# Two linear-attention branches under one gate: pk^T x of both branches as one 2x2 block product with seven block products

## The chip, the cores and the metric

The kernel runs on one core of a Trainium2 chip. The metric is the device time of one execution in microseconds. The engines are named as the profile names them: PE multiplies matrices (PEld is its weight load), DVE does vector arithmetic, ACT activations and copies, POOL little here, and SP issues nearly all DMAs. SBUF is the memory that all engines and the DMAs reach, PSUM the one that matmuls write into.

## The reference

```python
x = A_x                                        # 2048 x 640; B_x is not used
g = sigmoid((x * gate_w).sum(-1, keepdims=True))
def branch(x, wqkv, wo):                       # S=2048, D=640, H=32 heads of Dh=20
    q, k, v = split_heads(x @ wqkv)
    phi = lambda t: where(t > 0, t + 1, exp(t)) + 1e-6
    pq, pk = phi(q), phi(k)
    kv  = einsum("bhsd,bhse->bhde", pk, v);  z = einsum("bhsd->bhd", pk)
    num = einsum("bhqd,bhde->bhqe", pq, kv); den = einsum("bhqd,bhd->bhq", pq, z) + 1e-6
    return merge_heads(num / den) @ wo
out = g * branch(x, A_wqkv, A_wo) + (1 - g) * branch(x, B_wqkv, B_wo)
```

All inputs and the output are bf16. Both branches have the same x, so v is never formed: the kernel computes G = pk^T x (640 x 640 for each branch), and from it kv = G Wv, of which only the diagonal blocks of the heads are kept. The small kv and Wo are multiplied to one matrix W' for each branch, so that out = (pqA, scaled) W'A + (pqB, scaled) W'B.

## The kernel before, in words

Everything is laid out in SBUF by `body`, which builds a list of operations, each with an engine, a planned cost, its inputs and outputs, and a priority. A planner (`Sched`, L77 to L256) then walks through a modelled time: PE's operations keep the order in which the program lists them, the operations of the other engines are taken by the earliest modelled start and then by priority, and this order is emitted. Each engine then works through its own fixed list, waiting on semaphores. PSUM has eight banks of 512 fp32 columns, which the planner hands out (pool "ps").

The stages, in PE's order:

- **Loads** (L425 to L457, one SP queue in the program's order; x's tile 1 and the gate weights go by ACT's). The key weights, x transposed (XT, DMA transposes), x in rows (XN, with a column of ones behind its 640 columns), then WQ, WV and WO of both branches, and the constants CST last. WO is loaded in pieces of 60 partitions (L444 to L451).
- **Keys** (L592 `k_both`, for tiles 2 to 15 of 128 rows). One tile of both branches takes three PSUM banks: 512 columns of A, the last 128 of A and B together with a gate column, 512 of B. That is 15 matmuls at L613. ACT takes exponentials (L626, L630, L667); DVE clamps them (L640) and adds max(k, 0) from PSUM (L650). The result pk goes to PKS.
- **G and queries** (L713 `g_unit`, L870 `q_unit`). For each branch and each of five column groups g, 16 row tiles are accumulated: a matmul of 512 columns (L720) and one of 129 (L721; the last column is x's ones column, which gives z). Between them lie query units: five matmuls of 512 columns (L874), an exponential and a relu on ACT (L891, L898), a clamp and an addition on DVE (L901, L909). All of branch A is done before branch B. A G group is copied by ACT (L729) and transposed by a DMA on SP's queue into GS (L739).
- **Denominators** (L923 `t_sum`, L950 `den`). DVE multiplies pq by z and sums over five groups (L932, L935), a DMA transposes the sums, DVE reduces four rows to one (L969), takes the reciprocal (L981) and multiplies by the gate (L984), a DMA transposes back, and DVE scales pq (L1013). This is done in 512-row blocks b = 0 to 3 and for each branch by itself.
- **kv and W'** (L754 `kv_unit`, L804 `wp_burst`). kv is 30 matmuls for a branch (L782), masked by DVE into KVL (L762). A W' burst is half of the columns (L817), copied by ACT (L832); after the second half five DMAs store W' to memory (L854) and one reads it back in another layout (L846).
- **Output** (L1026 `o_mm`). 16 tiles; a tile has 10 matmuls of 512 columns and 10 of 128 for the two branches (L1034). For 15 tiles the part of branch A is done first (L1054 `o_part`), stored as fp32 by ACT, and added by DVE to the part of branch B (L1060 `o_rest`, L1071). The last tile is accumulated in PSUM. One DMA stores each tile.

The order around the change is written out by hand in L1119 to L1185: the fills of the B groups with queries, kv and W' of A inside B's G groups, the 15 `o_part` of A around kv and W' of B, and four `behind` relations.

```python
for g in range(NC):                        # L1119
    g_unit("A", g, lambda k: q_next(1))
...
for g in range(NC):                        # L1151
    g_unit("B", g, fill_b(g))
    q_next((2, 2, 1, 0, 0)[g])
...
l = PKt[X][:, t, g::5]                     # L719
e.matmul(a[:, 0:512], l, XN[:, t, 0:512], start=(t == 0), stop=(t == NT - 1))
return e.matmul(a[:, 512 : D + 1], l, XN[:, t, 512 : D + 1], start=(t == 0), stop=(t == NT - 1))
```

Of the kernel before, what the change touches and what calls it, by code (L numbers as in the profile page):

```python
# [39 lines left out]
XS_W = 672  # L40
KB_W = 648

# [222 lines left out]
def body(nc, A_x, A_wqkv, A_wo, B_x, B_wqkv, B_wo, gate_w, out, log=None):  # L265
# [11 lines left out]
    WKW = sb("WKW", [128, 2 * NU * D], bf)  # L277
    WKC = WKW[:, 0 : NC * 2 * KB_W].rearrange("p (c x f) -> p c x f", c=NC, x=2)
    WK = {X: WKC[:, :, i, :] for i, X in enumerate(XS)}
    WQ = {X: sb("WQ" + X, [128, NC, D], bf) for X in XS}  # L280
    WV = {X: sb("WV" + X, [128, NC, D + 28], bf) for X in XS}
    WO = {X: sb("WO" + X, [128, NU, D], bf) for X in XS}
    PKS = sb("PKS", [128, 2, NT * D], bf)
    PK = {X: PKS[:, i, :] for i, X in enumerate(XS)}
    PKt = {X: PK[X].rearrange("p (t f) -> p t f", t=NT) for X in XS}
    EX = [sb("EX%d" % i, [128, NC, 512], bf) for i in range(3)]

    def slot(X, i):
        return PK[X][:, 2560 * i : 2560 * i + 2560].rearrange("p (g s) -> p g s", g=NC)

    PQ = {
        ("A", 0): EX[0],
        ("A", 1): EX[1],
        ("A", 2): EX[2],
        ("A", 3): slot("A", 0),
        ("B", 0): slot("A", 1),
        ("B", 1): slot("A", 2),
        ("B", 2): slot("A", 3),
        ("B", 3): None,
    }  # L300
    GTS = {X: WKW[:, i * NU * D : i * NU * D + NC * D].rearrange("p (g f) -> p g f", g=NC) for i, X in enumerate(XS)}
    GS = {X: sb("GS" + X, [128, NC, D], bf) for X in XS}
    KVL = {X: sb("KVL" + X, [128, NU, GR], bf) for X in XS}
    WST = {X: WKW[:, i * NU * D : (i + 1) * NU * D].rearrange("p (u f) -> p u f", u=NU) for i, X in enumerate(XS)}
    WP = {X: sb("WP" + X, [128, NC, D], bf) for X in XS}
    XNf = XN[:, :, :].rearrange("p t f -> p (t f)")
    GSf = GS["A"][:, :, :].rearrange("p c f -> p (c f)")
    PQ["B", 3] = GSf[:, 0:2560].rearrange("p (g s) -> p g s", g=NC)
    FXT = {"A": WV["A"][:, :, :].rearrange("p c f -> p (c f)")[:, 0:2048].rearrange("p (b s) -> p b s", b=NB), "B": XNf[:, 0:2048].rearrange("p (b s) -> p b s", b=NB)}
    NOA = 15  # L310
    OA = [XNf[:, 2048 + 1280 * i : 3328 + 1280 * i].bitcast(f32) for i in range(6)]
    OA += [PK["B"][:, 1280 * i : 1280 * i + 1280].bitcast(f32) for i in range(8)]
    OA += [XT[:, :, :].rearrange("p c s -> p (c s)")[:, 0:1280].bitcast(f32)]
    NEK, NEQ, NOS = 4, 4, 4
    EK = sb("EK", [128, NEK, D], bf)
    EQ = EK[:, :, :].rearrange("p k f -> p (k f)")[:, 0 : NEQ * 512].rearrange("p (k f) -> p k f", k=NEQ)
    TSB = sb("TSB", [128, NB * 1024], bf)
    OST = TSB[:, 0 : NOS * D].rearrange("p (k f) -> p k f", k=NOS)
    TSF = [TSB[:, 1024 * b : 1024 * b + 1024].bitcast(f32) for b in range(NB)]
    TSH = sb("TSH", [128, NB, 512], bf)  # L320
    ZC = sb("ZC", [128, 2 * NC], f32)
    DNT = sb("DNT", [128, NB, 128], f32)
    TTR = sb("TTR", [128, NB, 4, 128], bf)
    FF = sb("FF", [128, NB, 512], bf)
# [3 lines left out]
    GG = sb("GG", [128, 2, NT], f32)  # L328
    ONE = sb("ONE", [128, 2], bf)
    SCR = sb("SCR", [128, 1], f32)  # L330
    EPSC = sb("EPSC", [128, 1], f32)
    PS = nc.alloc_psum_tensor("ps", [128, 8, 512], f32)


    IDN = sb("IDN", [128, 128], bf)
# [3 lines left out]
    sch = Sched({"ps": 8, "ek": NEK, "eq": NEQ, "os": NOS})  # L339
# [29 lines left out]

    def dve4(n):  # L370
        return 150 + 0.27 * n
# [25 lines left out]
    bpad = {X: Buf("pad") for X in XS}  # L397
    for X in XS:
        for lo, hi in ((0, 4), (D + 4, D + 28)):
            op("POOL", lambda e, X=X, lo=lo, hi=hi: e.memset(WV[X][:, :, lo:hi], 0.0), 300.0, outs=[bpad[X]], prio=10**6, name="wvpad")  # L400
    bxo = Buf("xo")
    op("POOL", lambda e: e.memset(XN[:, :, D : D + 1], 1.0), 200.0, outs=[bxo], name="xones")
# [36 lines left out]
    for X in XS:  # L439
        dma("SP", "wv" + X, WV[X][:, :, 4 : D + 4], w3(X, 2), 819200, outs=[bwv[X]])  # L440
    for X in XS:
        for r in range(2):
            bwo[X, r] = Buf("wo")
            dma(  # L444
                "SP",
                "wo%s%d" % (X, r),
                WO[X][4 + HR * r : 64 + HR * r, 0:5, :],
                wo[X][0:600, :].rearrange("(u r p) n -> r p u n", r=2, p=HR)[r],
                384000,
                outs=[bwo[X, r]],  # L450
            )  # L451
        bwo[X, 2] = Buf("wo")
        dma("SP", "wopad" + X, WO[X][0:4, 0:5, :], wo[X][0:4, :].unsqueeze(1).to_broadcast([4, 5, D]), 25600, outs=[bpad[X]])
        dma("SP", "wo2" + X, WO[X][64:104, 5, :], wo[X][600:640, :], 51200, outs=[bwo[X, 2]])

    dma("SP", "cst", CST[:, :], cap[:, :], 128 * CW * 2, outs=[bcst])
    loading.clear()  # L457


# [50 lines left out]
    def gate_col():  # L510
        bt = Buf("gwp", "ps")

        def tv():
            return PS[:, bt.slot, 0:NC]

        op("PE", lambda e: e.matmul(tv(), GWZ[:, :], IDN[:, 0:NC], start=True, stop=True), 60.0, ins=[bgw, bid], outs=[bt], name="gwt")
        op(
            "DVE",
            lambda e: e.tensor_copy(WKC[:, :, :, D : D + 1], tv().unsqueeze(2).unsqueeze(3).to_broadcast([128, NC, 2, 1])),
            170.0,  # L520
            ins=[bt],
            outs=[bgc],
            name="gwc",
        )


    bpk = {}

# [21 lines left out]
    def k_post(X, t, ps):  # L550
        ek = Buf("ek", "ek")
        ek2 = Buf("ek2")
        pk = Buf("pk%s%d" % (X, t))
        bpk[X, t] = pk
        first = []
        if X == "B":
            b = Buf("ge")
            bge.append(b)
            op(
                "ACT",  # L560
                lambda e: e.activation(GE[:, t : t + 1], psw(ps, D + 1)[:, D : D + 1], ACT.Exp, scale=-1.0),
                200.0,
                ins=[ps],
                outs=[b],
                name="ge",
            )
            first = [b]
        op("ACT", lambda e: e.activation(EK[:, ek.slot, :], psw(ps, D), ACT.Exp), act_cost(D), ins=[ps] + first, outs=[ek], name="ke")
        op(
            "DVE",  # L570
            lambda e: e.tensor_scalar(EK[:, ek.slot, :], EK[:, ek.slot, :], 1.0, EPS, op0=ALU.min, op1=ALU.add),
            dve4(D),
            ins=[ek],
            outs=[ek2],
            name="kt",
        )
        op(
            "DVE",
            lambda e: e.scalar_tensor_tensor(PKt[X][:, t, :], psw(ps, D), 0.0, EK[:, ek.slot, :], op0=ALU.max, op1=ALU.add),
            dve1(D),  # L580
            ins=[ps, ek, ek2],
            outs=[pk],
            name="ks",
        )

    def k_unit(X, t):
        ps = Buf("k", "ps", 2)
        for c in range(NC):
            k_step(X, t, c, ps)
# [635 lines left out]
```

## Time and profile before

| what | us |
|---|---|
| time, median of 3 runs (lowest, highest) | 187.42 (187.31, 187.66) |
| span of the profiled execution, the time that the profile gives of it | 186.2 |
| first matmul of the key tiles from 2 on (L613) | 10.36 |
| first matmul of the G groups (L720) | 48.33 |
| first output matmul (L1034) | 137.88 |
| last engine instruction (DVE, L1078) starts | 184.17 |
| PE busy in these three stretches, 10.36:48.33, 48.33:90.00, 108.00:137.88 | 37.76, 41.41, 29.67 |
| DVE busy in the same | 32.34, 23.93, 28.01 |
| ACT busy in the same | 24.47, 21.26, 20.42 |

How to read it: the span goes from the first to the last instruction of the profiled execution; the time of a run is a little longer than the span. An engine's busy time is the union of its instructions. A matmul's length in the profile holds the way through the array, which the next matmul overlaps, so the distance from one start to the next tells what it costs. The chain of work that ended last goes back from the last instruction, at each step to what released it. A group of instructions is one source line with one operation and, by shape, one form; "idle before" is the time for which its engine had nothing to do just before, with the engine and line that ended it.

### The profile page before, as it was taken

To read this page: it belongs to the slowest core of one execution; us is meant where nothing else is said; L and a number is where in the kernel's file an instruction comes from. 1 tells how busy PE (TensorE), PEld (TensorE's weight loads), DVE (VectorE), ACT (ScalarE), POOL (GpSimd) and SP (SyncE) were. 2 spreads that over 40 slices of the span, in tenths; PEclk is the share of its full clock that TensorE was granted. 3 is DMA by queue.
4 is the path that set the end of the run, shared out by engine and by line. 5 is a ranking of instruction groups with operands and counts; after the bars stand their busy time and mean duration, and the time that the engine had idled before them with its cause. 6 is when DMAs were issued, how large, how long until landed. Compare 5 with 4: busy or idle time off the path is not lost.

```text
span 186.2 us, 3116 instructions
## 1 busy us (share of the span) xinstructions
PE 182.4 (98%) x1204; PEld 105.8 (57%) x1227; DVE 137.2 (74%) x278; ACT 96.6 (52%) x181; POOL 1.1 (1%) x12
## 2 busy tenths in 40 slices
PE   9999999999999999999999999999999999999995
PEld 4555555555655556555556555555566555555553
DVE  2289888888733555487989899999899998159563
ACT  5265656666554546544675666888623784400001
POOL 2000000000000000000000000000000000000000
PEclk9999999999999999999999999999999999999999
DMA  7979999998006011010501402115515246622324
GB/s 225 268 150 144 273 364 369 353 179 159 4 0 39 0 35 35 4 35 6 114 0 39 84 10 56 32 43 168 178 39 118 58 77 175 189 74 110 138 108 141
DMA packets 36501, 21.37 MB, mean 115 GB/s; under 512 B 25694, under 2 KB 36230, under 8 KB 36486
## 3 DMA queue, kind: packets, MB, share of 16 engines
q1 hardware_dynamic: 36188, 20.97, 44.9%
q10 hardware_dynamic: 298, 0.20, 0.4%
q8 instruction: 9, 0.15, 0.3%
q14 instruction: 6, 0.05, 0.1%
HBM read 10.87 MB, written 4.26 MB: 81 GB/s over the span
## 4 chain that ended last, share of the span: by engine, by line
PE 93%; SPq 3%; DMA 2%; issue 1%; DVE 0%; DVEq 0%
PE ps L1034 23%; PE ps L874 23%; PE ps L613 20%; PE ps L720 18%; PE ps L721 5%; SPq L353 3%; DMA XT<-in_A_x_dram 2%; PE ps L782 2%; PE ps L817 1%; PE ps L535 0%; PE ps L536 0%; DVE TSB L1078 0%; DVEq L237 0%
## 5 line engine op out<-in xcount | busy, mean ns | idle before, releaser
L720 PE MATMUL ps<-XN,PKS 128*128 128x512 bf16 x154 | 45.8, 379 | 0.1
L891 ACT ACTIVATE EK<-ps 128x512 bf16<-128x512 f32 x40 | 23.9, 598 | 30.1 <-PE ps L874 27.0
L613 PE MATMUL ps<-WKW,XT 128*128 128x512 bf16 (+1 forms) x206 | 37.9, 343 | 0.2
L721 PE MATMUL ps<-XN,PKS 128*128 128x129 bf16 x160 | 35.2, 220 | 0.3
L613 PEld LDWEIGHTS ps<-WKW,XT 128*128 128x128 bf16 x210 | 20.3, 97 | 17.5
L720 PEld LDWEIGHTS ps<-XN,PKS 128*128 128x128 bf16 x160 | 18.8, 117 | 15.8
L650 DVE SCALAR_TENSOR_TENSOR PKS<-ps,EK 128x512 bf16<-128x512 f32 (+1 forms) x42 | 24.0, 599 | 1.0
L874 PE MATMUL ps<-XT,WQA 128*128 128x512 bf16 x98 | 24.2, 379 | 0.1
L874 PE MATMUL ps<-XT,WQB 128*128 128x512 bf16 x97 | 23.4, 380 | 0.2
L901 DVE TENSOR_SCALAR EK<-EK 128x512 bf16<-128x512 bf16 x40 | 11.5, 288 | 14.0 <-ACT EK L891 13.8
L721 PEld LDWEIGHTS ps<-XN,PKS 128*128 128x128 bf16 x160 | 18.8, 117 | 3.0
L1034 PE MATMUL ps<-WPA,EX 128*128 128x128 bf16 (+1 forms) x117 | 16.6, 297 | 0.3 <-issue 0.2
L1034 PE MATMUL ps<-WPB,PKS 128*128 128x512 bf16 (+1 forms) x117 | 16.3, 297 | 0.2
L874 PEld LDWEIGHTS ps<-XT,WQB 128*128 128x128 bf16 x100 | 10.9, 118 | 8.6 <-issue 0.4
L874 PEld LDWEIGHTS ps<-XT,WQA 128*128 128x128 bf16 x100 | 10.6, 117 | 8.1
L1034 PEld LDWEIGHTS ps<-WPB,PKS 128*128 128x128 bf16 x120 | 9.3, 98 | 7.2
L1034 PEld LDWEIGHTS ps<-WPA,EX 128*128 128x128 bf16 x120 | 9.1, 98 | 7.1 <-issue 0.4
L1080 ACT ACTIVATE TSB<-ps 128x512 bf16<-128x512 f32 x1 | 0.6, 597 | 21.9 <-PE ps L1034 21.9
L898 ACT ACTIVATE PKS<-ps 128x512 bf16<-128x512 f32 x20 | 11.9, 594 | 0.0
L640 DVE TENSOR_SCALAR EK<-EK 128x768 bf16<-128x768 bf16 (+1 forms) x28 | 9.0, 321 | 3.9 <-ACT EK L630 3.9
L667 ACT ACTIVATE EK<-ps 128x512 bf16<-128x512 f32 x14 | 8.4, 597 | 6.6 <-PE ps L613 6.6
L626 ACT ACTIVATE EK<-ps 128x512 bf16<-128x512 f32 x14 | 8.4, 597 | 6.4 <-PE ps L613 6.4
(80 smaller groups left out, 200.7 us busy)
## 6 DMA issues: line engine op xcount, KB each, us to landing
out_dram<-TSB SPq DMA_DIRECT2D x15, 160.0 KB, 1.8
XN<-in_A_x_dram SPq DMA_DIRECT2D x1, 2240.0 KB, 9.5
WKW<-in_A_wqkv_dram SPq DMA_DIRECT2D x5, 160.0 KB, 3.5
WKW<-in_B_wqkv_dram SPq DMA_DIRECT2D x5, 160.0 KB, 3.6
WQA<-in_A_wqkv_dram SPq DMA_DIRECT2D x1, 800.0 KB, 11.1
WQB<-in_B_wqkv_dram SPq DMA_DIRECT2D x1, 800.0 KB, 12.3
WVA<-in_A_wqkv_dram SPq DMA_DIRECT2D x1, 800.0 KB, 11.8
WVB<-in_B_wqkv_dram SPq DMA_DIRECT2D x1, 800.0 KB, 13.2
```

What stands on the lines that cost most here:

```text
L613: x = e.matmul(two() if i == 1 else bank(i), XT[:, c, 128 * t : 128 * t + 128], r, start=(c == 0), stop=(c == NC - 1))
L626: op("ACT", lambda e: e.activation(ekw(0, 512), bank(0), ACT.Exp), act_cost(512), ins=[ps[0]], outs=[ek, ea], name="ke")
L640: lambda e: e.tensor_scalar(ekw(lo, hi), ekw(lo, hi), 1.0, EPS, op0=ALU.min, op1=ALU.add),
L650: lambda e: e.scalar_tensor_tensor(dst, src(), 0.0, e1(), op0=ALU.max, op1=ALU.add),
L667: op("ACT", lambda e: e.activation(ekw(768, 1280), bank(2), ACT.Exp), act_cost(512), ins=[ps[2]], outs=[ek, eb], name="ke")
L720: e.matmul(a[:, 0:512], l, XN[:, t, 0:512], start=(t == 0), stop=(t == NT - 1))
L721: return e.matmul(a[:, 512 : D + 1], l, XN[:, t, 512 : D + 1], start=(t == 0), stop=(t == NT - 1))
L874: r = e.matmul(PS[:, ps.slot, :], WQ[X][:, c, g::5], XT[:, c, 512 * b : 512 * b + 512], start=(c == 0), stop=(c == NC - 1),)
L891: lambda e: e.activation(EQ[:, eq.slot, :], PS[:, ps.slot, :], ACT.Exp),
L898: op("ACT", lambda e: e.activation(PQ[X, b][:, g, :], PS[:, ps.slot, :], ACT.Relu), act_cost(512), ins=[ps], outs=[rq], name="qr")
L901: lambda e: e.tensor_scalar(EQ[:, eq.slot, :], EQ[:, eq.slot, :], 1.0, EPS, op0=ALU.min, op1=ALU.add),
L1034: r = e.matmul(a[:, l0 - lo : h0 - lo], PQ[X, b][:, g, 128 * (t % 4) : 128 * (t % 4) + 128], WP[X][:, g, l0:h0], start=(X == first and g = ...
```

## The change

Pairs of row tiles (2j, 2j+1) and the two halves of x's columns make a 2x2 block product: with A1, A2, B1, B2 the pk of the two branches in even and odd tiles, and l, r the left and right 320 columns of x, G of A and of B is

the block matrix [A1^T A2^T; B1^T B2^T] times [x1l x1r; x2l x2r], summed over j and made with seven products of 320 or 321 columns instead of eight. For this

- DVE makes four sums of pk (S1 to S4, in PKS, which now has seven regions) and four sums of x's halves (TX), with low priority in the key stage;
- the key stage takes each branch in two matmuls of 512 and 128 (B: 129) columns, 20 a tile; ACT takes max(k, 0) for A in all tiles and for B in six odd ones (`RELUB`), so DVE adds in bf16;
- a G group now gives both branches. Three PSUM banks hold the products; ACT copies partial sums to PT, DVE adds them into the G tiles, and two DMAs transpose these;
- WV and WO are no longer loaded at the start, because their place is now taken by PKS regions; they are loaded in group 4, Wv after P2, Wo after P6;
- queries: 20 units of blocks 0 and 1 lie in and before the groups; those of blocks 2 and 3 come after the groups, two at a time, with exponentials and relus of 1024 columns; their pq lies where S1 and S3 were;
- kv and W' of both branches come after the groups, between the queries; denominators and scalings take both branches at once (1024 columns, 2560 columns);
- the output is accumulated in PSUM for both branches, without the fp32 parts and DVE's additions; only tiles 0 and 1 begin with A.

The diff, cut to its core:

```diff
+RELUB = (3, 5, 7, 9, 11, 13)
+QPRE = 2
+QO = 3
+NEA = 2
+QFILL = ((3, 2, 1, 1), (0, 1, 1, 1), (0, 1, 1, 1), (0, 1, 1, 1), (0, 1, 1, 0))
...
+    def load_wv(after):
+        for X in XS:
...
+            dma("SP", "wv" + X, WV[X][:, :, 4 : D + 4], w3(X, 2), 819200, outs=[bwv[X]], after=after, prio=-1)
+    def load_wo(after):
...
+                    WO[X][4 + HR * r : 64 + HR * r, 0:5, :],
+                    wo[X][0:600, :].rearrange("(u r p) n -> r p u n", r=2, p=HR)[r],
...
+    def s_pair(j):
...
+                out=PKS[:, RS1 : RS3 + 1, j, :],
+                in0=PKS[:, RB1, j, :].unsqueeze(1).to_broadcast([128, 2, D]),
+                in1=PKS[:, RB2 : RA1 + 1, j, :],
+                op=ALU.subtract,
...
+        for src, sub, dst, out, need in ((RA1, RS1, RS2, bs2, bs1), (RA2, RS2, RS4, bs4, bs2)):
...
+                    out=PKS[:, dst, j0 : j + 1, :], in0=PKS[:, src, j0 : j + 1, :], in1=PKS[:, sub, j0 : j + 1, :], op=ALU.subtract
...
+    def t_all(j0, j1):
...
+        tt(0, xr(0, j0, j1), xl(0, j0, j1), ALU.subtract, [])
+        tt(1, tk(0), xr(1, j0, j1), ALU.add, [0])
+        tt(2, xr(0, j0, j1), xr(1, j0, j1), ALU.add, [])
+        tt(3, xl(1, j0, j1), tk(1), ALU.subtract, [1])
...
+    for t in range(2, NT):
+        k_both(t, "AB" if t in RELUB else "A")
+        if t % 2:
+            s_pair(t // 2)
+    t_all(0, 8)
...
+                    r = e.matmul(PS[:, ps.slot, 0:w], PKS[:, reg, j, g::5], mov(j, w), start=(first and j == 0), stop=(j == 7), skip_group_check=not first)
...
+        prod(g, "P1", px, RA1, xv(0, False), W, True, ...)
+        s1 = save(t1, px, HC, "p1s")
+        prod(g, "P2", py, RA2, xv(1, False), HC, True, ...)
+        comb(ga, 0, py, t1, "c11")
+        fill(0)
+        prod(g, "P5", pz, RS1, tv(0), W, True, ...)
+        s5 = save(t5, pz, W, "p5s")
+        prod(g, "P6", px, RS2, tv(1), W, False, ..., after=[s1])
+        s2 = save(t2, px, W, "u2s")
+        fill(1)
+        prod(g, "P7", px, RS3, tv(2), W, False, ..., after=[s2])
+        c22 = comb(gb, HC, px, t5, "c22")
+        zb = zsum("B", px, t5, [c22])
+        prod(g, "P3", pz, RS4, xv(1, True), W, False, ..., after=[s5])
+        c12 = comb(ga, HC, pz, t2, "c12")
+        zsum("A", pz, t2, [c12])
+        fill(2)
+        prod(g, "P4", px, RB2, tv(3), HC, False, ..., after=[c22, zb])
+        op("ACT", ... GT[:, gb.slot, 0:HC], PS[:, px.slot, 0:HC], ACT.Copy ...)
+        for X, b in (("A", ga), ("B", gb)):
+            dma("SP", "gs%s%d" % (X, g), GS[X][:, :, 128 * g : 128 * g + 128], ..., transpose=True, prio=-2)
+        fill(3)
...
+    def fill_g(g):
+        def f(k):
+            if g == 4 and k == 0:
+                load_wv([last["P1"], last["P2"]])
+            if g == 4 and k == 1:
+                load_wo([last["P6"], last["P2"]])
+            q_next(QFILL[g][k])
+            ts_ready()
+        return f
+    q_next(QPRE)
     for g in range(NC):
...
+        g_unit(g, fill_g(g))
...
+    den(0)
+    q_next(2)
+    kv_unit("A")
     kv_unit("B")
...
+    q_next(1)
+    wp_burst("A", 0)
+    q_next(1)
+    den(1)
+    wp_burst("A", 1)
+    q_next(1)
+    ts_ready()
     wp_burst("B", 0)
...
+    q_next(1)
     wp_burst("B", 1)
...
+    q_next(QO)
+    early = [Buf("o", "ps", 2) for _ in range(NEA)]
+    for t in range(NEA):
+        o_mm("A", t, early[t], 0, D)
+    for t in range(NT - 1):
+        if t < NEA:
+            o_mm("B", t, early[t], 0, D)
+            o_post(t, early[t], 0, D, "ACT")
+        else:
+            out_unit(t)
+        if qs:
+            q_next(1)
+            if not qs:
+                den(2)
+                ts_ready()
+                den(3)
```

Here `W` is 321 and `HC` 320; a `q_next(1)` after the groups is a double unit. The waits after `load_wv` and `load_wo` are for the products named.

## The prediction, as it was put on record

> **What bounds the kernel now.** I read the page's first two parts, then the chain of work that ended last, then that chain in order of time, then the groups by shape, and the DMA views last.
>
> ```profile
> span 186.2 us, 3116 instructions
> ...
> PE 182.4 (98%) x1204; PEld 105.8 (57%) x1227; DVE 137.2 (74%) x278; ACT 96.6 (52%) x181; POOL 1.1 (1%) x12
> ...
> DVE  2289888888733555487989899999899998159563
> ...
> PEclk9999999999999999999999999999999999999999
> ```
>
> PE is busy in every slice at full granted clock, DVE is nearly full from slice 20 to 33, ACT is not. A busy PE may still not stream, so the chain in order of time:
>
> ```profile
> 98.23 0.22 PE ps L720
> 98.45 0.06 PE ps L721
> 98.50 0.22 PE ps L720
> ...
> 99.32 1.08 PE ps L874 x5
> 100.40 1.43 PE ps L782 x30
> ```
>
> A product step (512 columns, then 129) takes 0.272 us, a query unit (five of 512) 1.08, and 30 matmuls of at most 120 columns, each with a weight load, 1.43, or 48 ns each. These are rates of a stream, not latencies: PE is the bound, and from 10.4 to 184.2 us it hardly stops. So columns taken off PE come off the time one for one, and every new wait of PE is added one for one.
>
> **What the products save.** Before: 160 steps x 0.272 = 43.5 us. A 512-column matmul advances PE by 0.216 and a 129-column one by 0.056, hence 0.42 ns a column; 321 columns take 0.136. After: 5 groups x 7 products x 8 = 280 x 0.136 = 38.1. Gain **5.4 us**. The key projection takes 20 matmuls for two branches, not 15: 10 x 0.216 + 10 x 0.056 = 2.72 against 2.71 a tile, x14 = **+0.1**. Queries, kv, W' and output keep their matmuls.
>
> [...]
>
> **Sums on DVE before the products.** From the shapes 128x512 (424 ns) and 128x1280 (817) a bf16 addition costs 162 ns + 0.512 per column. The eight combinations each of S1/S3 and S2/S4 take 16 x 0.82 = 13.1 us, the four of TX 4 x 1.48 = 5.9, the key tiles' own work 8 x 1.82 + 6 x 1.49 = 23.5 (clamp 0.51, addition 0.49, addition from PSUM 0.82): 42.5 us between 10.4 and the first P5. That comes at 48.5 + 2 queries + P1 + P2 + 3 queries = 56.1, so 45.7 us are there. ACT takes 2.3 to 3.0 us a tile, mean 2.59, against 2.72 on PE. Inside a group P7 waits for U2's copy (0.2 + 0.44 us) behind one query (1.08), and P4 for c22 and z (1.6) behind P3 and a query (2.2). All is hidden, barely. If the cover is gone: 3 us. I take **+0.6**, ends 0 and 3.
>
> **The moved weight loads.** Call T the end of the last product: 48.5 + 2.2 (two queries) + 38.1 + 18 queries x 1.08 + 0.6 = 108.8 us. Wv and Wo now lie where PKS regions were: Wv is issued after P2 of group 4, Wo after P6, all on SP's queue, and the transposes of the last G tiles come after them there.
>
> ```profile
> 28.00:37.00 9.00, 8.95 (x51) 4.85 (x50) 7.37 (x16) 5.95 (x15) 0.00 (x0) 1.00 1.07 364
> 37.00:44.00 7.00, 7.00 (x40) 3.66 (x38) 6.03 (x14) 4.04 (x10) 0.00 (x0) 1.00 1.08 192
> ```
> ```profile
> WPB<-wpsB SPq DMA_DIRECT2D x1, 800.0 KB, 4.5
> ...
> WOB<-in_B_wo_dram SPq DMA_DIRECT2D x2, 375.0 KB, 13.3
> ...
> CST<-kconsts SPq DMA_DIRECT2D x1, 8.0 KB, 11.2
> ```
>
> The last two columns of a window are the DMA engines' share and GB/s. Loads of 128 partitions ran at 364 GB/s; from 37 us, when only Wo was left, the engines were as busy but moved 192. CST, 8 KB issued at 36.7 behind Wo, landed 11.2 us later: what stands behind Wo on this queue waits for all of Wo. Now the same after the change. From P2's end to T lie five products and two queries, 5 x 1.09 + 2 x 1.08 = 7.6 us; Wv A lands 4.5 us after its issue at T-7.4, Wv B 819 KB / 364 = 2.25 later, at T-0.65. Wo then takes what it took from 37.0 to CST's landing at 47.9, 10.9 us, less about 1 for the overlap with Wv's landing: the last G A transpose lands near **T+9.2**. PE reaches the kv product of A after four queries, T+4.3. It waits **4.9 us**. Behind that instruction on PE stand all the rest; on DVE the masks (L762) and, in its fixed order, the denominators; on SP's queue the first denominator transpose. Low end: Wo at 364 GB/s, then it ends at T+4.0 and the transposes at about T+4.6, a wait of 0.3; high end: the transposes take their usual 2.6 us after Wo, 5.9. I take the row of the same transfer.
>
> [...]
>
> **ACT between the bursts.** Four times a double query unit and a W' burst now follow each other. PE: 2.16 + 0.53 = 2.69. ACT:
>
> ```profile
> L891 ACT ACTIVATE EK<-ps 128x512 bf16<-128x512 f32 x40 | 23.9, 598 | 30.1 <-PE ps L874 27.0 <-DVE PKS L909 1.2 <-remote 1.1
> L832 ACT ACTIVATE WKW<-ps 124x960 bf16<-124x960 f32 x8 | 7.3, 969 | 1.0 <-PE ps L817 1.0
> ```
>
> 1024 columns by these rows take 1.03, 0.93 when back to back; exp and relu 1.87, two copies 1.76: 3.63 us. ACT falls 3.7 us behind over four. A unit holds two of the eight PSUM banks and a burst four, so about one unit of lag is covered. Walking bank by bank I get PE waits of 0.4, 1.0 and 1.0: **+2.4**, ends 0 and 3.7.
>
> **The round trip of W' B.** In the trace:
>
> ```profile
> 150.10 1.83 ACT L832 ACTIVATE WKW<-ps 124x960 bf16<-124x960 f32 x2
> ```
> ```profile
> 151.43 3.04 SPq L353 DMA_DIRECT2D wpsB<-WKW  x5
> ...
> 157.03 0.35 SPq L353 DMA_DIRECT2D WPB<-wpsB  x1
> ```
>
> The burst ended at 150.0, the load landed at 157.03 + 4.5 = 161.5: 11.5 us. Before, the O matmuls of A covered it. After, three double units (6.5), two O matmuls of A (2.7) and one of ACT's waits (1.0) cover 10.2. **+1.5**, ends 0 and 2.5.
>
> **DVE at the end.** After T-1.2 DVE has sums of group 4 (2.7), ten double query units (10.4), masks (4.5), four denominators of 4.2 (16.7), sums of blocks 2 and 3 (13.5) and eight scalings of 2560 columns, 1.4 each (11.1): 59 us. Block 3's first scaling then ends near 107.6 + 59 - 1.4 + 2 us of early idle time + two exposed transposes of 2.5 = 172. PE reaches output tile 12 at T + 20 queries (21.6) + kv (2.9) + bursts (2.1) + 12 tiles x 2.72 = 168.0 without waits, and at 176.8 with mine. So DVE is hidden in my forecast; it is what is late next.
>
> **Sum.** 186.2 - 5.4 + 0.1 + 0.6 + 4.9 + 2.4 + 1.5 = 190.3 us of span. The profile gives its execution's span, no other time; the median of the runs, 187.42, lies 1.2 above it. 190.3 + 1.2 = **191.5 us**.
>
> **Rivals.**
> Faster: Wo goes through at 364 GB/s or the transposes pass it, so kv waits 0.3 at most. For: the row cannot say why Wo was slow. Against: CST. Then 191.5 - 4.6 = 186.9, and with half of ACT's wait gone 185.7; below that DVE holds: tile 12 at 172, four tiles of 2.72, 2.0 to the end of the span, 1.2: 186.1, or 185.2 if one transpose is hidden. I say 186.0. It decides when the kv wait is under some 0.8 us.
> Much slower: DVE falls behind. The first products lose their 3 us instead of 0.6, and the kv wait leaves DVE, in its fixed order, idle as long, so that tile 12 comes at 172 + 4.9 + 2.4 = 179.3 and not at 176.8 + 2.4: 191.5 + 2.4 + 0.1 = 194.0, and up to 197.3 with the high ends of kv (1.0), ACT (1.3) and W' (1.0). I say 195. For: DVE is at nine tenths now. Against: 5 us lie between 172 and 176.8.
> Cancelled: the kv wait is about 2 us, ACT's 1: 187.2.
> Narrow products that do not stream at 0.136 us would undo the change; the 48 ns row excludes it.
> [...]
>
> **Chances.** Forecast (189 to 194): 0.58. Faster: 0.27. Much slower: 0.09. Cancelled: 0.06, mostly within the bound. This gives faster by over 0.2% (which is about what a measurement of this kernel tells from none) 0.27, within 0.05, slower 0.68. The range reaches from the rival's 185.4 to 194.5, the forecast's high ends taken singly; both signs are in it, and the forecast alone would have 189 to 194.
>
> **What the profile after would show.** Products: 280 matmuls at 0.136 us, 7.6 us a group. No idle time of PE before the first P5. Then one idle stretch of PE of about 5 us before the kv matmuls, ended by the DMA into GSA, with Wo landing just before; PE waits of about 1 us between the W' bursts, ended by ACT; one of about 1.5 before the first O matmul of B, ended by WPB. I am wrong if the kv wait is under 2 us, if PE waits in the key stage, or if output tiles wait for the scaling on DVE.

## The result, and the profile after

| | before | after |
|---|---|---|
| time, median (lowest, highest), us | 187.43 (187.31, 187.66), 4 runs | 198.66 (198.0, 199.73), 4 runs |
| ratio of the times | | 1.0604 [1.0566, 1.0643] |
| profiled execution: time, span, us | 186.2 of span | 198.07, 196.7 |

Line numbers in this part are those of the kernel after; the names are the same. The kernel became 6% slower, 11.2 us; the prediction had said 191.5, at most 194.5. (A ratio stands with its 95% interval in brackets.) The profiled spans differ by 10.5 us. From the first two parts of the page after:

```profile
span 196.7 us, 3099 instructions
...
PE 181.2 (92%) x1235; PEld 114.2 (58%) x1257; DVE 135.4 (69%) x230; ACT 105.9 (54%) x177; POOL 1.2 (1%) x12
...
DVE  2388969889898727282865717969999799543500
...
PEclk9999999999999999999999975999996999999999
```

PE was busy for 98% of the span, now for 92%, and the row PEclk has two dents that it did not have: the clock granted to PE fell twice. Where PE waits, its timeline says; the bracket at the end of a line is the idle time ahead of it and what ended it:

```profile
117.55 2.83 PE L924 MATMUL ps<-GSA,PKS 128*128 128x120 bf16 x30 [4.59 <-DMA GSA<-WKW]
...
128.91 1.03 PE L762 MATMUL ps<-XT,WQA 128*128 128x512 bf16 x4 [0.56 <-ACT PKS L785]
...
132.23 2.35 PE L762 MATMUL ps<-XT,WQA 128*128 128x512 bf16 x10 [0.67 <-ACT PKS L785]
...
136.03 2.11 PE L762 MATMUL ps<-XT,WQA 128*128 128x512 bf16 x9 [0.92 <-ACT PKS L785]
...
150.33 2.45 PE L1116 MATMUL ps<-PKS,PQ 128*128 128x128 bf16 x9 [5.16 <-DMA PKS<-wpsB]
```

kv (L924) waits 4.59 us for the transpose into GS, the units between the W' bursts (L762) 2.15 us for ACT in three waits, the first output product of B (L1116) 5.16 us for W' B: 11.9 us, against hardly any before. The clock, by windows (the third number from the end is the granted clock):

```profile
117.50:122.10 4.60, 4.55 (x50) 4.58 (x51) 3.23 (x4) 0.00 (x0) 0.00 (x0) 0.50 0.50 103
...
149.40:152.80 3.40, 2.47 (x10) 1.42 (x12) 3.16 (x8) 1.02 (x1) 0.00 (x0) 0.50 0.40 77
```

Behind each of the two long waits PE worked at half its clock, 4.55 and 2.47 us. I count half of that, 3.5 us, as lost, an estimate from the clock of 0.50 in these windows and from the 30 kv matmuls, which advanced PE by 1.43 us before and by 2.66 here. And the products, from the chain of work in order of time:

```profile
98.79 4.40 PE ps L806 x32
```

Four products of eight matmuls take 4.40 us, 0.1375 a matmul; 280 make 38.5 us against 43.5 before. So -5.0 for the products, +0.1 for the key stage, +11.9 of waits and +3.5 of half clock: 10.5, the whole difference of the spans.

Why W' B was late is read from SP's queue. The second number is how long the issue took:

```profile
103.22 1.57 SPq L366 DMA_DIRECT2D PKS<-in_A_wo_dram  x4
104.83 1.59 SPq L366 DMA_DIRECT2D PKS<-in_B_wo_dram  x4
107.72 2.16 SPq L366 DMA_TRANSPOSE GSA<-WKW  x1
...
139.19 1.25 SPq L366 DMA_TRANSPOSE XN<-XN  x1
140.48 3.14 SPq L366 DMA_DIRECT2D wpsB<-TX  x5
145.43 0.35 SPq L366 DMA_DIRECT2D PKS<-wpsB  x1
```

And what the two operations at 139.19 and 140.48 needed, on DVE and on ACT:

```profile
137.94 1.22 DVE L1064 TENSOR_TENSOR XN<-XN,GG 128x1024 bf16<-128x1024 f32 x1
```
```profile
135.49 1.96 ACT L972 ACTIVATE TX<-ps 124x960 bf16<-124x960 f32 x2
```

ACT had copied W' B at 137.45, but the stores (wpsB) stand on SP's queue behind the transpose back of the second denominator, which waited for DVE's L1064 until 139.16 and took 1.25 us to issue: the stores began 3.0 us after their data was there.

### The profile page after: what moved, and what is told of

Read it like the earlier page. It is cut to its first block, busy times and chain, and to the rows that moved or that the text cites. A ratio compares the mean times of both kernels' runs of the same rounds, so it can differ in the third digit from the quotient of the medians.

```text
span 196.7 us, 3099 instructions
## 1 busy us (share of the span) xinstructions
PE 181.2 (92%) x1235; PEld 114.2 (58%) x1257; DVE 135.4 (69%) x230; ACT 105.9 (54%) x177; POOL 1.2 (1%) x12
## 4 chain that ended last, share of the span: by engine, by line
PE 81%; DMA 8%; ACT 6%; DVE 1%; issue 1%; SPq 0%; DVEq 0%; ACTq 0%
PE ps L1116 21%; PE ps L806 18%; PE ps L557 17%; PE ps L762 15%; PE ps L558 5%; DMA GSA<-WKW 5%; ACT TX L972 3%; PE ps L924 3%; DMA PKS<-wpsB 2%; ACT EQ L784 2%; ACT PKS L785 2%; PE ps L486 1%; DMA wpsB<-TX 1%; PE ps L499 1%; DVE WKW L833 0%
## 5 line engine op out<-in xcount | busy, mean ns | idle before, releaser
L557 PE MATMUL ps<-WKW,XT 128*128 128x512 bf16 x154 | 43.8, 386 | 0.0
L784 ACT ACTIVATE EQ<-ps 128x512 bf16<-128x512 f32 (+1 forms) x30 | 22.5, 750 | 38.3 <-PE ps L762 31.6
L558 PE MATMUL ps<-WKW,XT 128*128 128x128 bf16 (+1 forms) x160 | 35.5, 222 | 0.3
L1116 PE MATMUL ps<-PKS,PQ 128*128 128x512 bf16 (+1 forms) x157 | 23.0, 307 | 5.3 <-DMA PKS<-wpsB 5.2
L1140 ACT ACTIVATE TX<-ps 128x640 bf16<-128x640 f32 (+1 forms) x16 | 11.2, 698 | 28.4 <-PE ps L1116 28.4
L597 ACT ACTIVATE EKT<-ps 128x640 bf16<-128x640 f32 x32 | 22.3, 704 | 6.9 <-PE ps L558 6.3
L762 PE MATMUL ps<-XT,WQA 128*128 128x512 bf16 x95 | 22.8, 380 | 2.3 <-ACT PKS L785 2.2
L806 PE MATMUL ps<-TX,PKS 128*128 128x321 bf16 (+1 forms) x160 | 24.6, 300 | 0.0
L762 PE MATMUL ps<-XT,WQB 128*128 128x512 bf16 x95 | 22.8, 379 | 0.3
L1116 PE MATMUL ps<-PKS 128*128 128x128 bf16 (+1 forms) x157 | 21.7, 298 | 0.2
L806 PEld LDWEIGHTS ps<-TX,PKS 128*128 128x128 bf16 x160 | 18.8, 117 | 5.0
L1116 PEld LDWEIGHTS ps<-PKS,PQ 128*128 128x128 bf16 x160 | 12.8, 101 | 15.2 <-DMA PKS<-wpsB 5.1
L806 PE MATMUL ps<-XN,PKS 128*128 128x321 bf16 (+1 forms) x120 | 18.0, 300 | 0.0
L1116 PEld LDWEIGHTS ps<-PKS 128*128 128x128 bf16 x160 | 12.3, 98 | 9.7 <-DVE PKS L1094 0.3
L762 PEld LDWEIGHTS ps<-XT,WQA 128*128 128x128 bf16 x100 | 11.5, 119 | 10.6 <-ACT PKS L785 2.4
L762 PEld LDWEIGHTS ps<-XT,WQB 128*128 128x128 bf16 x100 | 11.6, 118 | 8.2 <-issue 0.2
L806 PEld LDWEIGHTS ps<-XN,PKS 128*128 128x128 bf16 x120 | 14.1, 117 | 3.1
L828 ACT ACTIVATE EKT<-ps 128x321 f32<-128x321 f32 (+1 forms) x15 | 6.6, 439 | 11.2 <-PE ps L806 11.1
```

Of the source, the lines that this page charges most:

```text
L557: e.matmul(a[:, 0:512], l, WK[X][:, c, 0:512], start=(c == 0), stop=(c == NC - 1))
L558: return e.matmul(a[:, 512:w], l, WK[X][:, c, 512:w], start=(c == 0), stop=(c == NC - 1))
L597: op("ACT", lambda e, i=i, ps=ps: e.activation(ev(i), psw(ps, D), ACT.Exp), act_cost(D), ins=[ps] + first, outs=[ek, b], name="ke")
L762: r = e.matmul(PS[:, ps.slot + i, :], WQ[X][:, c, g::5], XT[:, c, 512 * b : 512 * b + 512], start=(c == 0), stop=(c == NC - 1),)
L784: op("ACT", lambda e: e.activation(ev(), pv(), ACT.Exp), act_cost(512 * n), ins=[ps], outs=[eq], name="qe")
L806: r = e.matmul(PS[:, ps.slot, 0:w], PKS[:, reg, j, g::5], mov(j, w), start=(first and j == 0), stop=(j == 7), skip_group_check=not first)
```

## The experiments

Every kernel from here on has each DMA transpose replaced by a plain DMA copy of the same bytes, between the same tiles and on the same queue, so its output is not the reference's. No run of these edits with the transposes exists, so what they show holds for the result itself only as far as the copies behave like the transposes. Times are medians; a ratio is against before, run beside it.

### The copies alone: p_before, p_after

```diff
-e.dma_start(d, src, transpose=transpose)
+e.dma_start(d, src)        # the source's dimensions regrouped to the target's shape
```

> The kernel before with each DMA transpose replaced by a plain DMA copy of the same bytes between the same tiles, on the same queue and in the same order, so the data in XT, GS, TTR and FXT are not transposed and the output is not the reference's. A control for the other runs with plain copies. Both theories expect that PE stays the bound and nothing waits: 186 to 188 us, clock 1.0.

> The changed kernel with each DMA transpose replaced by a plain copy of the same bytes, as in p_before; output not the reference's. Theory (the copies of the last G tiles wait in the queue behind Wo, whatever they are): PE's wait before kv stays at 4 to 5 us, the clock falls to half behind it, PE waits about 2 us in sum for ACT between the W' bursts and 4 to 5.5 us for the load of W' B: 196 to 199.5 us. Rival (the transposes themselves are slow there): the wait before kv falls under 1.5 us and the time to 190 us or less.

Measured: p_before 187.29 us, ratio 1.000 [0.9987, 1.0014]; p_after 196.32, 1.0473 [1.0416, 1.0531]. Before loses nothing by it, and after keeps what is to be explained: kv waits 4.60 us, half clock follows from 115.9 to 122.8, ACT's three waits are 0.56, 0.67 and 0.92. One thing is smaller: W' B is waited for 2.59 us, not 5.16, and no half clock follows there. The stores of W' B began at 137.8 and not at 140.5: DVE's L1064 ended 1.9 us earlier, at 137.25, and the back copy behind it took 0.47 us to issue and not 1.25. So experiments are read against 196.3, but the four runs of p_after lie between 195.1 and 197.2, and the profile is of the fastest: a difference of 1 us from 196.3 cannot be told from this scatter.

### Is it the shape of the Wo loads, their source, their queue? p1_wo120, f2_src, f3_wopool

Wo loaded in one piece of 120 partitions for a branch; read from other memory; issued by POOL:

```diff
-for r in range(2): dma("SP", WO[X][4 + HR * r : 64 + HR * r, 0:5, :], wo[X][0:600] ... 60 rows each)
+dma("SP", WO[X][4:124, 0:5, :], wo[X][0:600] ... 120 rows)      # p1_wo120
+... wqkv[X][0:600, 0:D] ...                                     # f2_src
+dma("POOL", ...)                                                # f3_wopool, all eight
```

> As p_after, with one edit: Wo is loaded with one DMA of 120 partitions for each branch instead of two of 60; every other instruction and every order stays. Theory (Wo is slow because of the 60 partitions that a DMA of it fills; the G copies stand behind it; late denominators that follow from this wait hold up the stores of W' B): Wo lands near 112 us instead of 116.7, PE's wait before kv falls under 0.8 us, the half clock behind it goes, and the wait for W' B falls to 2 to 3 us: 186.5 to 188.5 us. Rival (Wo is slow because of where it is read from): its rate stays near 190 GB/s and the time stays within 1 us of p_after.

> Leaves out: transposes as plain copies; and the 600 rows of Wo are read from the first 640 columns of wqkv in place of wo, so the output is not the reference's. Same tiles, partitions, bytes, queue and order as p_after (196.3 us). Theory A (the low rate of the Wo loads, 190 GB/s, comes from how wo lies in memory: rows of 1280 bytes directly behind each other): the loads run at about 360 GB/s, Wo has landed about 4 us earlier (112.5 us and not 116.4), the wait before kv is under 1.5 us, there is no half clock: 189 to 191 us. Theory B (it comes from the place in SBUF, or from the moment): Wo lands at 116 to 117 us, kv waits 4.6 us, 196.3 us.

> Leaves out: transposes as plain copies. Edit: the eight Wo loads go by POOL's queue and not by SP's; all else keeps its order. Theory 1 (the copies into GS wait because they stand behind Wo on SP's queue): they land 2 to 3 us after their issue, the wait before kv is under 0.8 us, no half clock, so 196.3 - 4.6 - 2.8 = 189 us, with up to 2 us more if Wo now lands after the first W' burst wants it. Rival (the DMA engines are full, so the copies wait whichever queue they are in): kv waits 3 us or more, 194 to 196 us.

Measured: 195.45 us (1.0442 [1.04, 1.0485]), 195.63 (1.0445 [1.0425, 1.0465]), 195.96 (1.0463 [1.0445, 1.0481]). In all three the last of Wo lands at 116.5 to 117.3 us (116.4 in p_after), and kv waits 5.0, 4.8 and 5.25. So neither the 60 partitions nor the source makes Wo slow. The third is the surprise. POOL's issues and, from the chain of work, the copy into GS, now with nothing but Wv ahead of it on SP's queue:

```profile
102.92 2.83 POOL L366 DMA_DIRECT2D PKS<-in_A_wo_dram  x4 [2.03 <-PE ps L806]
105.75 2.67 POOL L366 DMA_DIRECT2D PKS<-in_B_wo_dram  x4
```
```profile
107.14 10.36 DMA GSA<-WKW
```

It still takes 10.36 us and lands at 117.50, just after the last of Wo, though the last 50 KB of Wo were issued 0.7 us behind it. My theory of SP's queue falls in this form: the copy waits for Wo whichever queue Wo is in. Of the DMA queues that carry data, from 107.2 to 112 us only POOL's moved packets (their number, MB, share of 16 engines' time):

```profile
q0 software_dynamic: 314, 1.03, 101.7%
```

Why SP's packets did not move in that time is open.

### Take the half clock away: p2_fill, f1_fill

Matmuls that nothing reads keep PE busy where it waited, 21 before kv of A (both), and in p2_fill 23 more before the first output product of B:

```diff
 q_next(2)
+keep_busy(21)          # matmuls of 512 columns of a constant
 kv_unit("A")
```

> As p_after, with 21 matmuls of 512 columns of ones, whose result nobody reads, ahead of kv of A, and 23 ahead of the first output matmul of B; PE is then busy in both waits, and what it waits for is unchanged. Theory (an idle time of several us lets the clock fall to half for the work behind it): granted clock 1.0 throughout, 2.3 us less behind the first wait and 1.2 behind the second, 3 to 4 us less than p_after. Rival (the half clock has another cause, such as short matmuls or the DMA traffic): clock still 0.97 and the time within 1 us of p_after.

> Leaves out: the DMA transposes are plain copies of the same bytes, as in p_after (196.3 us). Edit: 21 matmuls of 512 columns that nothing reads stand on PE before the kv product of A, so that PE does not idle there; nothing is put anywhere else. Theory 1 (PE's clock is halved because PE idles 4.6 us): no half clock after 115 us, the two kv products take some 2.9 us and not 5.1, PE gets out of this stretch 2.3 to 3 us earlier: 193.3 to 194.2 us. Rival (the half clock comes from the kind of work there, or from the DMA traffic, and not from the idle time): half clock from 116 us as before, and the filling matmuls run into it: 196.3 us or more.

Measured: p2_fill 204.11 us (1.0896 [1.0865, 1.0928]). Its first filling works: no half clock there, and from kv's start to the next query 3.1 us pass and not 5.7. Its second one waited 6.5 us for a PSUM bank that ACT held, ran into half clock and cost some 8 us: it tells nothing of W' B. f1_fill has the first alone: no half clock until 146 us, though the kv matmuls and the DMAs beside them are the same, so it was the idle time (4.60 us in p_after) that brought it. But the time is 196.17 us (1.0467 [1.0411, 1.0523]), not the 193.3 to 194.2 expected; its four runs go from 194.6, at full clock throughout, to 197.0. The chain of work in order of time says why:

```profile
109.25 9.81 DMA XN<-XN
...
136.38 1.22 DVE XN L1064
...
140.56 2.69 DMA wpsB<-TX
...
147.92 2.44 PE ps L1116 x9
```

The chain no longer goes through PE. The copy of the first denominator (XN<-XN) stands behind Wo as well and lands at 119.06; DVE, in its fixed order, waits for it, then works almost without a break to L1064; the back copy on SP's queue waits for that, the stores of W' B behind it. The first output product of B starts at 147.92, at the same time as in p_after (147.86), f2_src (148.00) and f3_wopool (148.09). PE came earlier and waited longer, 3.76 us, and got its half clock there. A wait that is removed is no gain while a second chain ends at the same time.

### Out of the queue's way: f4_woafter, g2_tt

f4_woafter issues Wo after the last copies into GS. g2_tt also puts it behind the copy of the first denominator, and gives Wo's four pad rows a buffer of their own, which only the W' bursts wait for:

```diff
+for o in wo_ops: o.behind = gs_op["B", 4]      # f4_woafter
+for o in wo_ops: o.behind = tt_op[0]           # g2_tt, in its place
-dma("SP", "wopad" + X, ..., outs=[bpad[X]])    # g2_tt; kv waits for bpad
+dma("SP", "wopad" + X, ..., outs=[bwopad[X]])
```

> Leaves out: transposes as plain copies. Edit: the Wo loads stay on SP's queue but are issued after the copies into GS of the last group; DVE's order behind them shifts a little. Theory 1 (queue order): the copies land 2 to 3 us after their issue, kv waits under 0.8 us, no half clock; Wo then lands some 10 us later than its first issue, at 118 to 120 us, and the copy of the first denominator stands behind it. 189 us, up to 191 where the first W' burst waits for Wo. Rival (the engines are full either way, or Wv is what holds the copies back): kv waits 3 us or more, 194 to 196 us.

> Leaves out: transposes as plain copies. Edits to p_after (196.3 us): the Wo loads are issued on SP's queue after the copies into GS of group 4 and after the first copy of a denominator, and kv no longer waits for the four pad rows of Wo, only the W' bursts do. Theory 3 (everything that stands behind Wo in the DMA engines is late: first GS, then, where that is covered as in f1_fill, the denominator that DVE waits for, and through DVE's and SP's order W' B): kv waits under 0.8 us, there is no half clock, DVE goes on at 112.5 us and not at 119, W' B is back near 140 us and not 147.6: 196.3 - 7.8 = 188.5 us, 187.5 to 190. Rival (W' B is held by something else: first output product of B at 147.9 us whatever comes before, as in p_after, f1, f2 and f3): 195 to 196 us. Second rival: Wo itself is now late, the first W' burst waits for it by 3 us or more, 191 to 193 us.

Measured for f4_woafter: 195.25 us (1.0425 [1.0399, 1.0451]). The copies land 2.4 us after their issue, at 109.9 and 111.3: what they had waited for was Wo. And yet kv waits:

```profile
117.12 2.28 PE L924 MATMUL ps<-GSA,PKS 128*128 128x120 bf16 x30 [4.42 <-DMA PKS<-in_A_wo_dram]
121.40 1.86 PE L924 MATMUL ps<-GSB,PKS 128*128 128x120 bf16 x17 [2.00 <-DMA PKS<-in_B_wo_dram]
```

A second wait stood behind the first: kv needs the zero columns of Wv, and in the program they and the pad rows of Wo are one buffer (`bpad`, L459 and L477, waited for at L933), so kv waited for a piece of Wo that it never reads. I had not seen this wait. In g2_tt, 193.14 us (1.0293 [1.0248, 1.0338]), both are gone: kv starts without a wait and without half clock, and PE gets to the first output product of B 6.7 us earlier than in p_after. Not the 188.5 expected: W' B is back at 142.4 and PE, now early, waits for it 4.12 us and then works 6.8 us at half clock:

```profile
142.68 1.95 PE L1116 MATMUL ps<-PKS,PQ 128*128 128x128 bf16 x9 [4.12 <-DMA PKS<-wpsB]
```

### SP's order: g1_behind, g3_st

The five stores of W' B ahead of the back copy of the second denominator, on p_after (g1_behind) and on g2_tt (g3_st). DVE's order behind them shifts a little.

```diff
+ft_op[1].behind = last_st["B"]          # the back copy of denominator 1, the last store of W' B
```

> Leaves out: transposes as plain copies. One edit to p_after (196.3 us): the five stores of W' B are issued on SP's queue before the back copy of the second denominator, not after it. DVE's later order shifts a little. Theory 2 (the late first output product of B comes from SP's fixed order: in p_after ACT has copied W' B at 137.5 us, the stores start at 137.8 behind the back copy of 137.3, which waits for DVE): the stores start right after ACT's copies, W' B is back 0.3 to 1 us earlier than 147.6, 195.3 to 196 us. Rival (the stores wait for ACT alone): nothing changes, 196.3 us.

> Leaves out: transposes as plain copies. As g2_tt, and the stores of W' B before the back copy of the second denominator on SP's queue, as in g1_behind. Theory 2 with 3: another 0.3 to 1 us less than g2_tt, 187.0 to 188.2 us. Rival (the stores wait for ACT alone): the same as g2_tt.

Measured: g1_behind 194.52 us (1.0371 [1.0335, 1.0407]), the stores start at 136.7 and not at 137.8, the wait for W' B is 1.33 and not 2.59, though kv in this execution waited 1.1 longer than in p_after. g3_st 187.77 (1.002 [0.9992, 1.0048]): level with before, 8.6 us under p_after and 5.4 under g2_tt, of which I had expected 0.3 to 1. The stores start at 130.1 (132.8 in g2_tt), W' B is back at 139.5 (142.4), and the wait for it is 1.10 us, too short here to cost the clock, which is full throughout the profiled execution (two of the ten runs, 189.8 and 190.9 us, have a mean clock of 0.991 and 0.982):

```profile
139.73 1.30 PE L1116 MATMUL ps<-PKS,PQ 128*128 128x128 bf16 x9 [1.10 <-DMA PKS<-wpsB]
```

So two edits of order and one buffer of its own give back what the change lost. Alone they gave back 1.8 and 3.2 us, together 8.6. The traces fit this: each alone left one wait with half clock behind it (kv's of 5.75 us in g1_behind, W' B's of 4.12 in g2_tt).

### What keeps the seven products from showing: g4_qo, h2_nea, h5_kv, h6_kvnea, i2_prionea, i3_prioqo

g3_st still waits 4 us. Four edits on it: the last query unit ahead of the output products (g4_qo), three output tiles begun with A and not two (h2_nea), a query unit between the two kv products (h5_kv), the last two together (h6_kvnea):

```diff
-QO = 3
+QO = 4                                          # g4_qo; den(2), den(3) stay behind tile 0
-NEA = 2
+NEA = 3                                         # h2_nea, h6_kvnea
 kv_unit("A")
+q_next(1)                                       # h5_kv, h6_kvnea
 kv_unit("B")
-q_next(1)
```

> Leaves out: transposes as plain copies. As g3_st, and all ten double query units before the output products (four of them, not three, between the last W' burst and the first output product), so that 2.2 us more of PE's work cover W' B's way to memory and back. Theory (what is left in g3_st are ACT's waits of 2.1 us and about 1.5 us for W' B, and DVE has 2 us in hand before tile 12): the wait for W' B goes, 186.0 to 187.0 us, level with before at 187.1 or a little under. Rival (DVE is the bound there: block 3's scaling comes late and PE waits before tile 12): 187.5 to 189 us.

> Leaves out: transposes as plain copies. As g3_st (187.8 us), with the part of A of three output tiles, not two, ahead of the first output product of B. Theory (the 1.10 us for which PE still waits for W' B there lacks cover, and nothing else): 1.36 us more of PE's work lie before it, the wait is under 0.2 us, 186.6 to 187.0 us. Rival (as in g4_qo, more work there only moves the wait to PSUM banks or to DVE): 187.8 us or more.

> Leaves out: transposes as plain copies. As g3_st (187.8 us), with one of the double query units between the kv products of A and of B and not behind them, so that ACT, idle for 3.1 us there in g3_st, has work. Theory (PE's waits of 0.88 and 0.92 us between the W' bursts are ACT's lag, and ACT gets 1.4 us of it back): these two waits shrink to 0.6 us together or less, 186.6 to 187.2 us. Rival (what ACT gains is lost behind DVE's masks, which the first W' burst then waits for): 187.8 us or more.

> Leaves out: transposes as plain copies. The edits of h2_nea and h5_kv together on g3_st (187.8 us). Theory: both gains, 185.4 to 186.4 us, which would be under before's 187.4. Rival (DVE's last scalings become the bound before tile 12, or the waits move to PSUM banks): 187 us or more.

All four missed: 193.18 us (1.031 [1.0281, 1.0339]), 194.05 (1.0331 [1.0305, 1.0356]), 192.35 (1.0221 [1.0181, 1.0261]), 195.45 (1.0416 [1.039, 1.0442]). In h5_kv the W' bursts waited for DVE's masks and for ACT (0.87 and 1.14 us) and W' B was waited for 2.68 us, near my rival. In the other three PE waits 6.5 to 7.0 us, and not for W' B: it waits among the output products of A, in g4_qo before those of the second tile, in h2_nea and h6_kvnea before those of the third. In h2_nea, PE (two tiles, then the wait), then ACT, then DVE:

```profile
135.33 2.88 PE L1116 MATMUL ps<-PKS,PQ 128*128 128x512 bf16 x20
145.23 5.39 PE L1116 MATMUL ps<-PKS,PQ 128*128 128x512 bf16 x20 [7.02 <-ACT EQ L784]
```
```profile
144.15 2.15 ACT L784 ACTIVATE EQ<-ps 128x1024 bf16<-128x1024 f32 x2 [7.13 <-DVE PKS L794]
```
```profile
138.65 2.88 DVE L1094 TENSOR_TENSOR PQ<-PQ,XN 128x2560 bf16<-128x2560 bf16 x2
...
143.42 0.69 DVE L794 TENSOR_TENSOR PKS<-PKS,EQ 128x1024 bf16<-128x1024 bf16 x1
```

PE waits for ACT to leave the PSUM banks, ACT for a free buffer of exponentials, and that for DVE's addition (L794, 143.42), which in DVE's fixed order stands behind 9.8 us of sums and scalings, the last of the latter at 138.65. Order or load? The last two kernels let DVE take the clamp and the addition of a query unit first:

```diff
-op("DVE", ..., name="qt")                       # and "qs"
+op("DVE", ..., name="qt", prio=None if b < 2 else -10)
```

> Leaves out: transposes as plain copies. As h2_nea (194.1 us: three parts of A ahead of the first product of B), and DVE now takes the clamp and the addition of a double query unit of blocks 2 and 3 before the sums and scalings that are ready at the same time. Theory (in h2_nea PE waited 7.0 us for ACT, ACT for the buffers of two exponentials, and these for DVE, which had sums and scalings of 10.9 us ahead of the addition in its order): the wait for ACT goes, W' B is covered, no half clock: 186.2 to 187.2 us, under before's 187.7. Rival (DVE is full, whatever its order: the scalings of blocks 2 and 3 come late instead, and PE waits before tile 8 or 12): 188 to 191 us.

> Leaves out: transposes as plain copies. As g4_qo (193.2 us: all double query units before the output products), with DVE's order changed as in i2_prionea. Theory: the wait of 6.5 us for ACT goes, W' B is covered by 2.2 us more of PE's work, 186.0 to 187.0 us. Rival (DVE is full): 188 to 191 us, with PE's waits before tile 8 or 12 or still at the first output product.

Measured: 186.94 us (0.9978 [0.996, 0.9996]) and 186.57 (0.996 [0.9946, 0.9974]), both a little under before's 187.4, and 7.1 and 6.6 us under h2_nea and g4_qo. It was the order. From the page of i3_prioqo, which is of the slowest of its twelve runs (187.42):

```profile
span 185.9 us, 3123 instructions
...
PE 179.5 (97%) x1257; PEld 111.5 (60%) x1257; DVE 134.9 (73%) x230; ACT 106.1 (57%) x177; POOL 1.2 (1%) x12
```

PE's waits are 1.46 us for a query's banks behind DVE's masks, 0.94 and 0.67 for ACT and 0.52 for W' B, 3.6 together of the 5.0 that the products save. But these waits alone are no longer the bound. The first scaling of block 2 ends at 161.87, PE waits 0.20 us for it before tile 8, and the chain of work that ended last runs back from there almost wholly over DVE (one copy of 3.5 us lies between) to 123.65, and from there to a denominator's copy that was issued behind Wo:

```profile
114.17 9.47 DMA XN<-XN
...
160.46 1.41 DVE PKS L1094
...
161.92 21.92 PE ps L1116 x160
```

By this chain, PE with shorter waits would only come to tile 8 earlier and wait there. This is the best version, with the copies in place of the transposes.

### The form of the Wo load: h4_wo128

On p_after, Wo as 128 partitions from partition 0, without pad rows:

```diff
+dma("SP", WO[X][0:128, 0:5, :], wo[X].rearrange("(u p) n -> p u n", p=128))
```

> Leaves out: transposes as plain copies; and Wo is loaded in another layout, so that W' is not the reference's: 128 partitions from partition 0, 819 KB for a branch, in place of two pieces of 60 partitions from partition 4 and 64, and without the pad rows. Else as p_after (196.3 us). Theory B1 (the 190 GB/s of Wo come from the form of the load: 60 or 120 partitions from partition 4, 15 engines): the loads run at about 360 GB/s like Wv, Wo has landed near 112.5 us and not 116.4, kv waits under 1.5 us, no half clock, 190 to 193 us. Theory B2 (they come from the moment or the place, not from the form): Wo lands at 116 to 118 us, kv waits 4.6 us or more, 196 us.

Measured: 193.47 us (1.0323 [1.0292, 1.0354]), between the two theories. Between the landing of Wv and of the last of Wo lie 6.3 us and not 8.3, kv waits 2.13 and there is no half clock behind it (W' B is then waited for 3.47 us, with half clock). A's 819 KB came in 2.4 us, 343 GB/s, B's with 51 KB beside it in 3.9, 224 GB/s. So the form, or the pad rows that went with it, is a part of it. While B's came in, the DMA engines moved 298 GB/s in all, so other transfers had a share; whether that is why B's stayed slow is open. On how many DMA engines a load ran, no run shows.

## Why the prediction was wrong, step by step

The sign was right, the size was not, and the time, 198.66 us, lay above the range. What failed is the round trip of W' B, sized 3.7 us too small, and the clock, left out of the sum, 3.5 us.

- **Products**, -5.4: -5.0. The short matmuls stream, at 0.1375 us against 0.136. The key stage was as forecast, and PE waited nowhere in it or in the groups, so of the 0.6 for the sums nothing came; the last product ended at 108.6 (T, forecast 108.8). That this fits so well is two misses, +0.4 and -0.6, that cancel.
- **kv**, +4.9: 4.59. Right in place, size and releaser: the transpose landed behind Wo, at T + 8.8. That Wo and the transposes are "all on SP's queue" was not the reason (f3_wopool), and a second wait lay under it (`bpad`). The choice of the row of the same transfer, 192 GB/s, was right. Why the rate is so low was shown only in part (h4_wo128): 120 partitions in one piece (p1_wo120) were no faster, the engines moved 184 to 207 GB/s between 108 and 116 us, against 189 to 222 in p_after.
- **ACT**, +2.4: 2.15, as 0.56, 0.67 and 0.92 for 0.4, 1.0 and 1.0.
- **The round trip of W' B**, +1.5, ends 0 and 2.5: 5.16. This step failed. Its cover was right: "three double units (6.5), two O matmuls of A (2.7) and one of ACT's waits (1.0) cover 10.2"; from the last burst's end at 135.11 to 145.17 it is 10.1. The trip was taken over from before as 11.5 us; it took 15.2, from 135.11 to 150.33. I had counted the kv wait's effect on DVE ("the denominators") and on "the first denominator transpose" and not followed it one step on: the second one stands on SP's queue ahead of W' B's stores, and came late by DVE's delay. That this cost 3.0 us is read from the queue in the result's trace. The runs show the mechanism with plain copies: from g2_tt to g3_st this order alone changes, the stores start 2.7 us earlier and the wait falls by 3.0, from 4.12 to 1.10. With the transposes it is not tested. I had followed Wo along SP's queue, and not W'.
- **The clock**, not in the sum: +3.5, 2.3 behind kv and 1.2 behind W' B. Before's trace could not size it: its granted clock is 1.00 in every window, and no wait of PE in it is longer than 0.3 us. Behind kv the half clock held for 6.8 us, and the loss was 2.3, by the estimate above. The wait in the sum was 4.9 us long; what the clock did behind it was in neither the sum nor the range.
- **DVE is late next**: not in the time of the result (the first scaling of block 3 at 183.5, just before PE reached tile 12), but its fixed order is in the chain of W' B, and once the order of Wo and of SP's queue was changed it was what held g4_qo and h2_nea, and what bounds i3_prioqo. None of the rivals had this mechanism: I looked for DVE's lateness at the scalings alone.

With a W' B wait of 1.5 us and full clock, 196.7 - 3.7 - 3.5 = 189.5 us of span would have been left, just under the forecast's 190.3; this is an estimate from the sums above, and no run shows it. The low end of the faster rival does not follow from its own terms (172 less a hidden transpose of 2.5 gives 183.6, and PE alone 185.7, where it has 185.2, and the range 185.4); nothing here hangs on it. What stays open: how the result itself, with transposes, would answer to the same edits, and the rate of Wo.

## What to carry to other kernels

When a change adds a wait of some us to the bounding engine, follow every engine that idles with it to the end of its own fixed list: the next loss is where its late result stands in front of something else in an in-order queue. Look also for the second wait under each first one, here a shared buffer name and a second chain ending at the same time: f1_fill filled the visible wait, f4_woafter took away what it was for, and the gains of 0.2 and 1.1 us are within the scatter of p_after. Order is cheap to change: with plain copies, changes of order and one buffer of its own were worth 9.8 us, from p_after's 196.3 to i3_prioqo's 186.6.

## What the runs showed of the hardware

- In the profiled executions PE's clock was halved at every wait of 2.68 us (h5_kv, W' B) or more, and at none of 2.59 (p_after, W' B) or less. It stayed so for about 3.4 or 6.8 us (in the result 6.8 from 115.3 behind kv's wait and 3.4 from 149.4 behind W' B's), and in h4_wo128 it began only 0.8 us after the wait had ended, at 145.2.
- A copy of 160 KB issued on SP's queue with nothing but Wv ahead of it there landed 10.4 us later, behind 1.7 MB that were issued on POOL's queue between 4.2 us before it and 0.7 us after it (f3_wopool); issued before them it took 2.4 us (f4_woafter).
